# A gated mix of memory attention and a SiLU feed-forward: four v products on unscaled float32 operands, the last segment's q first, and two sets of scheduling prices

## The chip, the core and the metric

The kernel runs on one core of one Trainium2 chip. The metric is the device time of one execution in microseconds (us). Three executions of the kernel before took 552.75, 551.69 and 554.92 us; the median is 552.75 us.

The core has a matrix engine (TensorE, PE in the profile, with its weight loads listed as PEld), VectorE (DVE), ScalarE (ACT), GpSimd (POOL) and a queue engine that mostly issues transfers (SyncE, SP). Each engine works through its own instructions in the order in which they were written; semaphores make one engine wait for another.

## The reference

The input x has 2048 rows of 448 numbers. Two branches are computed from it and mixed row by row.

```python
q, k, v = x @ wq, x @ wk, x @ wv          # 16 heads of 28, 4 segments of 512 rows
for s in range(4):
    p = softmax(q[s] @ k[s].T / sqrt(28) + mask)
    a_dot = p @ v[s]
    a_mem = (phi(q[s]) @ M) / (phi(q[s]) @ z + 1e-6)     # phi(t) = t + 1 if t > 0 else exp(t)
    o[s] = sig(beta) * a_mem + (1 - sig(beta)) * a_dot
    M, z = M + phi(k[s]).T @ v[s], z + sum(phi(k[s]))
a = o @ wo
b = silu(x @ w1) @ w2                      # 1792 hidden columns
g = sigmoid((x * gate_w).sum(-1))
out = g * a + (1 - g) * b
```

Memory M and z are those of the segments before, so segment 0 has no memory to read and segment 3 does not write one.

## The kernel before

**Arithmetic.** PE multiplies 16-bit operands here. Every float32 operand is first multiplied by a power of two that fits its largest value and then split into a high 16-bit part and a low one, the remainder. The product is then three matmuls per 128 rows of the contraction (high·high, high·low, low·high). As the contraction is 448 = 3·128 + 64, and the 64 rows hold high and low stacked, one product of a tile is 3·3 + 2 = 11 matmuls. `halves` (L584) makes the two parts: the high part on ACT, or for the first segment and the weights on ACT or DVE (L590, L592), and the low part on DVE in one instruction (L579) or on POOL in two (L581, L582), of which the first scales the raw data in place. `product` (L604) issues the 11 matmuls, all of them on line L612.

**Scales.** A scale needs the size of the whole matrix first. For x and the weights of q, k and v it comes from sums of squares (`squares`, L432, on ACT) or largest values (`size`, L422, on DVE), one small float32 matmul over the partitions (L460, called a guard below), and a chain of four small DVE instructions (L464 to L468). The last of them writes `up`, which the high and low parts wait for.

**Stages.** First the loads and scales of x's first segment and of wv, wq and wk. While they arrive, PE runs matmuls on a zeroed tile that nothing reads: 8 of them (L791), then 37 more (L796, `MORE`), each of lowest priority. Then the projection stage: for 16 pairs of segment and group of four heads, `proj` (L893) makes q and k, `vproj` (L955) makes v in 16 tiles of 128 rows, `memory` (L996) accumulates M, and `retrieve` (L1031) reads it with float32 matmuls (L1044, L1045) for segments 1 to 3. After it the attention of all segments, with 10 of the 14 column blocks of the feed-forward in between as filler, and at last the output stage: the other four blocks, `@ wo`, the mix and the stores.

**Order.** The instructions of all engines are put in order while the program is built, by a list scheduler in the file (`Sched`, L146). Each task has an engine or a choice of two, an assumed duration, a priority and the PSUM banks or buffers that it takes; of all tasks that can go, the one that starts first goes, and ties on PE are settled by priority plus a price for weight loads that nothing covers (`PRICE`, `rank`, L214). Numbers at the head of the file (L37 to L91) set priorities. `SLACK` biases the choice between two engines. `LOCK` stands for DVE and POOL keeping each other out of a shared port. PSUM has eight banks, in three groups: mm (q and k), sc (v, transposes, scores) and cc (guards, memory, retrieval). A product takes the next bank of its group and cannot begin until the bank's last reader is done.

**Names.** `raw` holds wv and wq as loaded, `wa` here wk, `xraw` a tile of x; `wvs`, `wqs`, `wks` and `xh` are the split forms; `vt` a finished tile of v; `stg` a finished q or k; `pe`, `pp`, `ph` its steps through phi; `tqk`, `spk`, `rv` small scale factors; `amr` what retrieval gives.

## Time and profile before

| | |
|---|---|
| median of three runs | 552.75 us |
| the profiled execution's own time | 552.3 us |
| its span, first to last instruction | 550.6 us |
| outside the span | 1.7 us |
| PE, PEld busy | 540.9, 301.6 us |
| DVE, ACT, POOL busy | 403.2, 407.4, 336.7 us |
| granted PE clock, mean | 1.000 |

The span is what the prediction works in; the profiled execution is 0.45 us below the median, and 1.7 us lie outside its span. A timeline row gives the start in the span, the time until the last instruction of the row ended, the engine, the source line, what is written and read, and how many instructions the row merges; behind it in brackets stands the idle time ahead of it and what ended it. Instructions of one engine overlap at their ends, so what one costs in a row of many is the distance between starts, which is shorter than the duration in a row of one.

### The profile page before, as it was taken

Reading aid. Unit: us, or ns where it says so; the run is one execution under the profiler, and the core shown is the slowest. Engines: PE = TensorE matmul, PEld = TensorE weight load, DVE = VectorE, ACT = ScalarE, POOL = GpSimd, SP = SyncE. Lnnn points to the kernel's source line nnn. Section 1 sums busy time; section 2 is a strip of 40 time slices with the busy share of each in tenths; the row PEclk is TensorE's granted clock in tenths of the full one; section 3 lists DMA queues with packets and bytes.
Section 4 is the critical chain, followed back from the end, with each engine's and each line's share of the span. In section 5 each row is a group of like instructions: output and inputs, shape, how many; then the busy total and the mean of one; then the engine's idle time right before and its main releaser. Section 6 shows DMA issues by size and latency. Waiting matters only on the chain.

```text
span 550.6 us, 11673 instructions
## 1 busy us (share of the span) xinstructions
PE 540.9 (98%) x4087; PEld 301.6 (55%) x4087; DVE 403.2 (73%) x991; ACT 407.4 (74%) x698; POOL 336.7 (61%) x543
## 2 busy tenths in 40 slices
PE   8999999999999999999999999999999999999997
PEld 3455566556644556555565555565555555555544
DVE  5998999797869866778655789767897228864472
ACT  5996888595457988999887999879997897501140
POOL 3115525526623788888899988798989886211220
PEclk9999999999999999999999999999999999999999
DMA  8678578455467324332324334465301212689972
GB/s 309 230 227 251 175 214 230 145 147 169 137 183 188 110 77 118 104 88 69 101 73 119 87 85 137 128 134 141 106 9 47 86 52 62 227 197 247 257 202 69
DMA packets 78059, 78.94 MB, mean 143 GB/s; under 512 B 44040, under 2 KB 67720, under 8 KB 78000
## 3 DMA queue, kind: packets, MB, share of 16 engines
q1 hardware_dynamic: 77424, 77.21, 49.3%
q10 hardware_dynamic: 576, 0.99, 0.5%
q8 instruction: 32, 0.52, 0.4%
q14 instruction: 27, 0.22, 0.1%
HBM read 48.41 MB, written 26.09 MB: 135 GB/s over the span
## 4 chain that ended last, share of the span: by engine, by line
PE 92%; ACT 4%; DVE 2%; DMA 2%; issue 0%; DVEq 0%; ACTq 0%
PE mm L612 30%; PE mm L1192 17%; PE sc L612 11%; PE sc L717 6%; PE sc L1288 6%; PE cc L1192 6%; PE cc L1322 6%; PE cc L612 5%; ACT pf L1293 2%; PE cc L1044 1%; DMA raw<-in_wq_dram 1%; ACT phl L1305 1%; PE cc L1007 1%; PE sc L946 1%; PE sc L713 1%; DMA raw<-in_wv_dram 1%
## 5 line engine op out<-in xcount | busy, mean ns | idle before, releaser
L1309 POOL TENSOR_TENSOR phl<-pf,phl 128x384 f16<-128x384 f32 (+1 forms) x192 | 188.8, 1003 | 25.8 <-ACT phl L1305 25.7
L1293 ACT ACTIVATE pf<-sc,lift,es 128x512 f32<-128x512 f32 (+1 forms) x192 | 126.2, 706 | 13.2 <-PE sc L1288 10.8
L727 DVE CUSTOM_DVE_ANT_0 sc<-sc,mk 128x384 f32<-128x384 f32 (+1 forms) x192 | 105.6, 573 | 27.5 <-PE sc L717 25.3
L1192 PE MATMUL mm<-wb,ghl 128*128 128x448 f16 (+1 forms) x516 | 112.0, 348 | 0.0
L612 PE MATMUL mm<-xh,wa 128*128 128x512 f16 x429 | 107.0, 378 | 0.0
L1192 PEld LDWEIGHTS <-ghl 128*128 128x128 f16 x684 | 64.5, 97 | 51.0 <-issue 0.4
L1305 ACT ACTIVATE phl<-pf 128x1280 f16<-128x1280 f32 x64 | 81.4, 1272 | 14.3 <-POOL pf L1299 13.9
L612 PEld LDWEIGHTS <-wa 128*128 128x128 f16 x572 | 53.8, 97 | 54.7 <-issue 1.8
L1288 PE MATMUL sc<-ring 86*128 86x512 f16 (+3 forms) x256 | 62.5, 299 | 0.6 <-DVE mx L727 0.5
L717 PE MATMUL sc<-ring 84*128 84x128 f16 (+3 forms) x256 | 59.4, 299 | 0.7 <-ACT pf L1293 0.6
L1322 PEld LDWEIGHTS <-phl 128*128 128x128 f16 x1280 | 42.0, 96 | 10.1
L612 PE MATMUL mm<-xh,wqs 128*128 128x512 f16 x176 | 43.2, 379 | 0.8 <-DVE wqs L579 0.8
L1322 PE MATMUL cc<-vg,phl 128*128 128x29 f16 (+1 forms) x1280 | 43.7, 182 | 0.0
L623 POOL TENSOR_TENSOR ol<-ol,ml 128x448 f32<-128x448 f32 x12 | 13.6, 1136 | 46.9 <-DMA ol<-o_scr 37.2
L612 PE MATMUL mm<-xh,wks 128*128 128x512 f16 x176 | 41.9, 379 | 0.0
L1330 DVE TENSOR_REDUCE oraw<-cc 128x116 f32<-128x232 f32 x64 | 25.3, 396 | 20.6 <-PE cc L1322 20.4
L629 ACT ACTIVATE oh<-ol,os 128x448 f16<-128x448 f32 x16 | 10.7, 666 | 39.2 <-POOL ol L623 39.2
L612 PE MATMUL sc<-wvs,xh 128*128 128x450 f16 x176 | 37.8, 353 | 0.2 <-ACT xh L590 0.2
L1192 PE MATMUL cc<-wb,ghl 128*128 128x448 f16 x168 | 37.7, 352 | 0.0
L612 PE MATMUL cc<-xh,wa 128*128 128x512 f16 x143 | 36.5, 378 | 1.1 <-DVE amr L1050 1.1
L1288 PEld LDWEIGHTS <-ring 86*128 86x128 f16 x256 | 24.2, 97 | 23.0 <-issue 1.1
L612 PE MATMUL sc<-wos,oT 128*128 128x448 f16 x176 | 35.7, 352 | 0.0
(177 smaller groups left out, 920.8 us busy)
## 6 DMA issues: line engine op xcount, KB each, us to landing
rawf<-in_w_dram SPq DMA_DIRECT2D x26, 256.0 KB
rawf<-in_w_dram SPq DMA_DIRECT2D x28, 224.0 KB
v_scr<-vt SPq DMA_DIRECT2D x16, 232.0 KB
vg<-v_scr SPq DMA_DIRECT2D x16, 232.0 KB
xraw<-in_x_dram SPq DMA_DIRECT2D x14, 256.0 KB
q_scr<-stg SPq DMA_DIRECT2D x16, 224.0 KB
ring<-q_scr SPq DMA_DIRECT2D x16, 224.0 KB
k_scr<-stg SPq DMA_DIRECT2D x16, 224.0 KB
```

The source lines that it names most:

```text
L612: nc.tensor.matmul(ps(), *p[i], start=(i == 0), stop=(i == n - 1))
L623: d = pool(530, lambda: nc.gpsimd.tensor_add(b.v, b.v, m.v), d, e, uses=[b, m], **k)
L629: hi = copy(D + 110, lambda: nc.scalar.activation(half2.v[:, :D], ol.v, AF.Copy, scale=sc), *ready, takes=[half2], uses=[ol], prio=prio)
L717: nc.tensor.matmul(ps.v[:, u:u + n], rg.v[:KS, 0, hh, i * 128:(i + 1) * 128], rg.v[:KS, 1, hh, :n], start=(i > 0), stop=(i > 0 or j == 3), ...
L727: nc.vector.tensor_tensor_reduce(r, r, MK[:, L - n:], 1.0, NEG, OP.add, OP.max, mx.v[:, hh, i:i + 1])
L1192: nc.tensor.matmul(ps.v[:, lo:hi], g.v[:, y, sl], w.v[:, z, lo:hi], start=(j == 0 and i == 0), stop=(j == len(fs) - 1 and i == 2))
L1288: nc.tensor.matmul(ps.v[:, e:e + w], rg.v[:KK, 1, hh, j * 128:(j + 1) * 128], rg.v[:KK, 0, hh, j * 128:], start=True, stop=True)
L1293: ex.append(sact(e, lambda b=b, ps=ps, pf=pf, e=e: nc.scalar.activation(pf.v[:, b, :e], ps.v[:, :e], AF.Exp, bias=lift, scale=es[:, s:s + ...
L1305: hi = copy(1280, lambda hl=hl, flat=flat: nc.scalar.activation(hl.v[:, 0], flat(), AF.Copy), *mk, takes=[hl], uses=[pf], prio=p0 + 2)
L1309: low = pool(w - u + 22, lambda hl=hl, flat=flat, u=u, w=w: nc.gpsimd.tensor_sub(hl.v[:, 1, u:w], flat()[:, u:w], hl.v[:, 0, u:w]), low, u ...
L1322: nc.tensor.matmul(p[:, i, :2 - z], hl.v[:, z, u:u + 128], vg.v[:, j, hh, :2 - z], start=(z == zs[0] and i == 0), stop=(z == zs[-1] and j ...
L1330: nc.vector.tensor_reduce(orw.v[:, hh], p, axis=AX.X, op=OP.add)
```

## The change

There are three parts, and some smaller ones with them.

**The first four v products.** For the 128-row tiles 0 to 3 the product is done by `vearly`: four float32 matmuls on the unscaled `xraw` and `raw`, as soon as these have landed. Scale and remainder are taken afterwards, by the factor `rvf` that the copies out of PSUM multiply with. The loads are put in another order for that: on SP x tile 0, wv slices 1 and 3, x tile 2, on ACT's queue wv 0 and 2, x 1 and 3. 27 of the 37 low-priority matmuls go. `wvs`, the split form of wv, is still needed for segments 1 to 3, but later; its high parts are all made on ACT.

**The last segment.** Priorities of its q products and of its retrievals are lowered step by step with the group (`LASTQ`), so that they come ahead of its k and v.

**Prices in two stages.** `PRICE` and `SLACK` have one value in the projection stage and another (`PRICE2`, `SLACK2`) afterwards, and nearly all the numbers that set priorities have new values.

Beside these: x's first-segment low parts are bound to an engine (tile 0 to POOL, the others to DVE), squares are always taken on ACT, DVE's high parts count as users of the shared port and POOL's small instructions no longer do, and the very last output tile is cut 336 + 112 columns wide where it was 224 + 224.

```diff
-MORE = 37
+MORE = 10
...
-PRICE = 124.57
+PRICE = 249.08
+PRICE2 = 142.57
+SLACK2 = -0.34
...
-    def halves(j, hi, lo, dst, src, n, d, prio, takes=(), uses=(), both=False):
+    def halves(j, hi, lo, dst, src, n, d, prio, takes=(), uses=(), both=False, after=None, on=None):
...
-        return [h, scaled(n + 64 * (len(lo) - 1), low, h, uses=tuple(takes) + tuple(uses), prio=prio)]
+        if on:
+            eng, m = (pool, 2.2) if on == "POOL" else (dve, 1)
+            return [h, eng(m * (n + 64 * len(lo)), lambda: low(nc.gpsimd if on == "POOL" else nc.vector), h, after, port=on == "DVE",
+                           uses=tuple(takes) + tuple(uses), prio=prio)]
+        return [h, scaled(n + 64 * (len(lo) - 1), low, h, after, uses=tuple(takes) + tuple(uses), prio=prio)]
...
-            XC[s, c] = halves(NSEG - 1 - s, hi, lo, lambda: X16[s], src, L, d, prio, uses=[b], both=s == 0)
+            XC[s, c] = halves(NSEG - 1 - s, hi, lo, lambda: X16[s], src, L, d, prio, uses=[b], both=s == 0,
+                              after=EARLY[c][1] if s == c == 0 else None, on=("POOL" if c == 0 else "DVE") if s == 0 else None)
...
+        def vearly(k, prio):
+            ps, p, (xr, dx) = Buf(BK["sc" if k < 3 else "mm"]), None, XR[0, k]
+            for c in range(NC + 1):
+                wr, view, dw = RAWW["v", c]
+
+                def go(c=c, view=view):
+                    w = 128 if c < NC else REM
+                    nc.tensor.matmul(ps.v[:, :D + 2], xr.v[:w, c * 128:(c + 1) * 128], view()[:w], start=c == 0, stop=c == NC)
+                p = pe(quad(D + 2), go, p, dx, dw, takes=[] if c else [ps], uses=[ps, xr, wr], prio=prio)
+            EARLY[k] = ps, p
...
-            p = product(lambda: ps.v[:, :D + 2], pairs, D, prio, deps=need, cuts=cuts, takes=[ps], kind=half)
+            if k < NF:
+                ps, p = EARLY[k]
+                fit, turn, known = rvf, -1.0, RVF[0]
...
-            proj(t, "q", o)
+            proj(t, "q", o if s < NSEG - 1 else o - LASTQ * g)
...
-                retrieve(t, o + 8)
+                retrieve(t, o + 8 if s < NSEG - 1 else o + 8 - LASTQ * g)
...
+    sch.price, sch.slack = PRICE2, SLACK2
...
-            halves = [(0, D // 2), (D // 2, D)] if tail and tb == TB - 1 else [(0, D)]
+            halves = [(0, 3 * D // 4), (3 * D // 4, D)] if tail and tb == TB - 1 else [(0, D)]
```

The order in which instructions stand changes on every engine. Line numbers of the changed kernel differ (L460 becomes L468, L579 L587, L581 and L582 L589 and L590, L612 L624, L796 L808, L977 L1001, L1044 L1068, L1050 L1074). At the start PE had, ahead of the first v product, low-priority matmuls and the third guard's followers:

```order
L460 MATMUL cc_264<-sums,ones_73 128x5
...
L796 LDWEIGHTS maskb
L796 MATMUL mm_141<-maskb 128x512
L612 LDWEIGHTS xh_96
L612 MATMUL sc_295<-wvs,xh_96 128x450
...
L612 LDWEIGHTS wqs
L612 MATMUL mm_347<-xh_96,wqs 128x512
```

Now it has the float32 products there, with the four guards between them, and low-priority matmuls ahead of the first q product. Names with mm are in the mm banks; the last float32 product takes one of them, and the first k product (`mm_397`) is the next to take the same bank.

```order
L808 MATMUL mm_143<-maskb 128x512
L978 MATMUL sc_193<-raw_120,xraw 128x450 x4
L468 MATMUL cc_213<-sums,ones_73 128x5
L978 MATMUL sc_215<-raw_120,xraw 128x450 x4
L468 MATMUL cc_239<-sums,ones_73 128x5
L978 MATMUL sc_241<-raw_120,xraw 128x450 x2
L468 MATMUL cc_257<-sums,ones_73 128x5
L978 MATMUL sc_241<-raw_120,xraw 128x450 x2
L978 MATMUL mm_273<-raw_120,xraw 128x450 x4
L468 MATMUL cc_306<-sums,ones_73 128x5
```

So 44 16-bit matmuls of v are gone from behind the scales, and 16 float32 ones stand ahead of them. DVE, which makes the low parts, had this between the scale of x's first segment and that of wk (the chain L464 to L468 for wk stands behind it):

```order
L579 SCALAR_TENSOR_TENSOR xh_96<-xraw,up,xh_96 64x128
L579 SCALAR_TENSOR_TENSOR wqs<-raw_119,up,wqs 128x512 x3
L428 TENSOR_REDUCE sizes<-wqs 128x1
L579 SCALAR_TENSOR_TENSOR wqs<-raw_119,up,wqs 128x512
L428 TENSOR_REDUCE sums<-xraw 128x1 x3
L464 TENSOR_REDUCE few_123<-cc_379 128x1
```

The same place on DVE now, from the chain of wq's scale on:

```order
L476 RECIPROCAL up<-top 128x1
L1001 SCALAR_TENSOR_TENSOR vt_107<-sc_193,rvf,vt_107 128x16x28
L1001 SCALAR_TENSOR_TENSOR vt_108<-sc_215,rvf,vt_108 128x16x28
L441 TENSOR_REDUCE sums<-xraw 128x1
L472 TENSOR_REDUCE few_124<-cc_306 128x1
L473 TENSOR_SCALAR few_124<-few_124 128x1
L475 TENSOR_SCALAR top<-few_124 128x1
L476 RECIPROCAL up<-top 128x1
L587 SCALAR_TENSOR_TENSOR wqs<-raw_120,up,wqs 128x512 x4
L587 SCALAR_TENSOR_TENSOR wks<-wa,up,wks 128x512 x4
L1001 SCALAR_TENSOR_TENSOR vt_109<-sc_241,rvf,vt_109 128x16x28
L1001 SCALAR_TENSOR_TENSOR vt_110<-mm_273,rvf,vt_110 128x16x28
```

The low parts of wq moved behind the chain of wk's scale, and the copies that free the float32 products' banks stand at two places, the last of them behind all low parts of wq and wk. POOL had only small instructions in that part of the program:

```order
L516 TENSOR_SCALAR tqk<-top 128x1
L813 AFFINE_SELECT maskb<-maskb 128x128
L514 TENSOR_SCALAR tqk<-top 128x1 x2
L516 TENSOR_SCALAR spk<-up 128x1
L514 TENSOR_SCALAR spk<-spk 128x1
```

It now has the low part of x's tile 0 and, behind the small ones, those of wv's four slices, two large instructions for each:

```order
L524 TENSOR_SCALAR rvf<-up 128x1
L589 TENSOR_SCALAR xraw<-xraw,up 128x384
L590 TENSOR_TENSOR xh_97<-xraw,xh_97 128x3x128
L589 TENSOR_SCALAR xraw<-xraw,up 64x128
L590 TENSOR_TENSOR xh_97<-xraw,xh_97 64x128
L522 TENSOR_SCALAR tqk<-top 128x1 x2
L524 TENSOR_SCALAR spk<-up 128x1
L522 TENSOR_SCALAR spk<-spk 128x1
L825 AFFINE_SELECT maskb<-maskb 128x128
L589 TENSOR_SCALAR raw_120<-raw_120,up 128x450
L590 TENSOR_TENSOR wvs<-raw_120,wvs 128x450
```

This is work that moved from DVE to POOL. At the end of the projection stage DVE had the two reductions of the last retrieval directly ahead of the feed-forward's first work:

```order
L977 SCALAR_TENSOR_TENSOR vt_113<-sc_2118,vt_113 128x16x28
L989 TENSOR_SCALAR gate<-gate 128x4
L990 RECIPROCAL gate<-gate 128x4
L991 TENSOR_SCALAR ogate<-gate 128x4
L1050 TENSOR_REDUCE amr<-cc_2150 128x232
L1050 TENSOR_REDUCE amr<-cc_2158 128x232
L1055 RECIPROCAL amw<-amw 128x16
```

There now stand a v tile and a k product's remainder behind them:

```order
L1074 TENSOR_REDUCE amr<-cc_2062 128x232
L1074 TENSOR_REDUCE amr<-cc_2077 128x232
L1079 RECIPROCAL amw<-amw 128x16
L1001 SCALAR_TENSOR_TENSOR vt_114<-sc_2071,vt_114 128x16x28
L1013 TENSOR_SCALAR gate<-gate 128x4
L1014 RECIPROCAL gate<-gate 128x4
L1015 TENSOR_SCALAR ogate<-gate 128x4
L920 SCALAR_TENSOR_TENSOR stg<-mm_2096,stg 128x512
```

On PE, 8 matmuls of v and 11 of k now stand between the last retrieval and the first feed-forward matmul, where none stood before.

More of the change, by code (lines that the diff above doesn't have):

```diff
@@ L158, in __init__ @@
         self.tail = 1.0
+        self.price, self.slack = PRICE, SLACK
     def add(self, eng, dur, fn, deps=(), takes=(), uses=(), prio=0.0, lat=0.0, port=False):
@@ L200, in locked @@
     def locked(self, t, eng, s):
-        if eng == "POOL" or eng == "DVE" and t.port:
+        if eng == "POOL" and t.port is not None or eng == "DVE" and t.port:
             s = max(s, self.port["DVE" if eng == "POOL" else "POOL"] + LOCK)
@@ L249, in run @@
                 t.end = s + t.costs[t.eng]
-            if t.eng == "POOL" or t.eng == "DVE" and t.port:
+            if t.eng == "POOL" and t.port is not None or t.eng == "DVE" and t.port:
                 self.port[t.eng] = t.end
@@ L434, in squares @@
         at, junk = place(j), Buf(JUNK[0])
[L436 to L443 removed]
+        SIZE[j].append(copy(n + 200 - 45, lambda: nc.scalar.activation(junk.v[:, :n], view(), AF.Square, accum_out=at), *deps,
+                            takes=[junk], uses=uses, prio=prio))
     def total(j, view, n, *deps, uses=(), prio):
@@ L509, in few @@
     def few(n, fn, *deps, **k):
-        return sch.add("POOL", 0.33 * n, fn, deps, **k)
+        return sch.add("POOL", 0.33 * n, fn, deps, port=None, **k)
     def by(o, i, a, b=None, op0=OP.mult, op1=OP.mult):
@@ L965, in pairs @@
-            def pairs():
-                p = passes(W["v"], X16[s][:, :, tb * 128:(tb + 1) * 128], True)
-                return [p[i] for i in order]
-            p = product(lambda: ps.v[:, :D + 2], pairs, D, prio, deps=need, cuts=cuts, takes=[ps], kind=half)
+            v = Buf(VT)
+            if k < NF:
+                ps, p = EARLY[k]
+                fit, turn, known = rvf, -1.0, RVF[0]
+            else:
+                ps = Buf(BK["sc"])
+                p = product(lambda: ps.v[:, :D + 2], lambda: passes(W["v"], X16[s][:, :, tb * 128:(tb + 1) * 128], True), D, prio,
+                            deps={c: WS["v"][c] + XC[s, c if s else tb] for c in range(NC + 1)}, takes=[ps], kind=half)
+                fit, turn, known = FIT, tqk[:, 3 * s + 2:3 * s + 3], VREADY[s]
```

122 lines of the change are left out of this document (61 added, 61 removed).

## Prediction

> **What bounds the kernel now.** I read the totals first, then the chain that ended last, then busy time by stretches, and at last what PE waits for.
>
> ```profile
> span 550.6 us, 11673 instructions
> PE 540.9 (98%) x4087; PEld 301.6 (55%) x4087; DVE 403.2 (73%) x991; ACT 407.4 (74%) x698; POOL 336.7 (61%) x543
> ...
> PE 92%; ACT 4%; DVE 2%; DMA 2%; issue 0%; DVEq 0%; ACTq 0%
> ```
>
> PE is busy for 540.9 of 550.6 us and carries 92% of the chain. Only two things can move the time: a change in PE's work, and the 9.7 us in which PE idles. The stretches show where those lie (columns: length, then busy us of PE, PEld, DVE, ACT and POOL).
>
> ```profile
> core 0: us, PE busy (x) PEld busy (x) DVE busy (x) ACT busy (x) POOL busy (x), PEclk, DMA share, GB/s
> 15.00:20.00 5.00, 4.20 (x21) 1.88 (x21) 4.74 (x12) 5.00 (x11) 0.95 (x2) 1.00 0.72 245
> 30.00:35.00 5.00, 5.00 (x27) 2.36 (x26) 4.90 (x13) 5.00 (x10) 1.46 (x6) 1.00 0.80 242
> 130.00:160.00 30.00, 28.61 (x171) 16.97 (x169) 20.76 (x41) 13.74 (x28) 16.78 (x34) 1.00 0.46 136
> 160.00:200.00 40.00, 38.80 (x278) 20.28 (x277) 33.65 (x84) 33.85 (x53) 21.53 (x30) 1.00 0.57 155
> 540.00:551.00 11.00, 6.89 (x49) 4.46 (x46) 2.86 (x5) 0.00 (x0) 0.00 (x0) 0.97 0.16 54
> ```
>
> PE idles 1.4 us at 130 to 160, 1.2 us at 160 to 200 and some 4 us in the tail; at 30 to 35 not at all, though DVE and ACT have almost no slack there. The granted clock is 1.00, so durations can be compared across stages. What ended the idle time after 60 us (matmul, what released it, us in all, count, longest):
>
> ```profile
> PE cc L612 <- DVE amr L1050: 1.1, 1, 1.1
> PE sc L717 <- ACT pf L1293: 0.6, 2, 0.3
> ...
> PE cc L1045 <- DVE phq L935: 0.3, 1, 0.3
> ```
>
> The first and the last belong to the last retrieval, ahead of the feed-forward. At the start, "busy" hides what counts, because PE runs matmuls that nothing reads. There the order of PE has to be read.
>
> ```profile
> 4.37 2.97 PE L796 MATMUL mm<-maskb 128*128 128x512 bf16 x13
> 7.26 0.39 PE L460 MATMUL cc<-sums,ones 128*128 128x5 f32 x2
> ...
> 11.46 0.39 PE L460 MATMUL cc<-sums,ones 128*128 128x5 f32 x2 [0.99 <-DVE sums L459]
> ...
> 15.13 3.98 PE L612 MATMUL sc<-wvs,xh 128*128 128x450 f16 x20 [0.22 <-ACT xh L590]
> 18.95 0.38 PE L612 MATMUL mm<-xh,wqs 128*128 128x512 f16 x1
> ...
> 20.14 2.58 PE L612 MATMUL mm<-xh,wqs 128*128 128x512 f16 x11 [0.81 <-DVE wqs L579]
> ```
>
> Until 15.13 us PE does nothing that is needed but guards. From 15.13 to 18.95 it does 20 of the first segment's 44 v matmuls, then waits for wq's low part, and from 20.14 on it has work without a gap. So the kernel's PE time is counted from 20.14: what must still be done then, plus the stalls behind it.
>
> **The change part by part.** *A, the removed v matmuls.* 44 go, but 20 of them ran before 20.14, in time that q could not use. So 24 are saved.
>
> ```profile
> 49.98 2.10 PE sc L612 x11
> ```
>
> This link of the chain is one product of 11 matmuls: 2.10 / 11 = 0.191 us each. A is −24 × 0.191 = −4.6 us.
>
> *The float32 products.* There is no float32 matmul with 450 columns before. The nearest rows are retrieval's, with 232 and 116 columns (starts, not lengths, are read):
>
> ```profile
> L460 PE MATMUL cc<-sums,ones 128*128 128x5 f32 x14 | 2.3, 234 | 1.3 <-DVE sums L459 1.0 <-ACT junk L438 0.3
> ...
> 127.61 0.46 PE L1044 MATMUL cc<-mhl,phq 112*128 112x232 f32 x1
> 127.91 0.22 PE L1045 MATMUL cc<-mhl,phq 112*128 112x116 f32 x1
> 127.97 0.33 PE L1044 MATMUL cc<-mhl,phq 112*128 112x232 f32 x1
> 128.13 0.22 PE L1045 MATMUL cc<-mhl,phq 112*128 112x116 f32 x1
> 128.19 0.26 PE L1007 MATMUL cc<-vt,phk 128*112 128x232 f16 x1
> ```
>
> A float32 matmul leaves two records (14 for seven guards, whose pairs take 2.3 / 7 = 0.33 us each). A record of 232 columns takes 128.13 − 127.97 = 0.16 us, one of 116 columns 0.06, so 450 columns give an estimate of 0.16 + 218 × 0.10 / 116 = 0.35, and two records 0.70 us per matmul. The bounds are 0.38 (two records at the 16-bit 0.19) and 1.03 (0.70 and a guard's whole pair on top, for weight loads that nothing covers); I take 0.70, worked out from the same kind of instruction. Sixteen cost 11.2 us and the four guards between them 1.3. When they can begin is seen on ACT, which starts on wv's first slice as it lands:
>
> ```profile
> 4.41 0.58 ACT L438 ACTIVATE junk<-raw 128x450 bf16<-128x450 f32 x1 [0.25 <-DMA raw<-in_wv_dram]
> ```
>
> With 0.4 us for x's first tile to follow, they go from about 4.8 to about 17.3 if no later load is late. They take the place of idle time and of the 27 unread matmuls (13 take 2.97 us), ahead of 20.14. The cover ends where DVE wants wk's guard, 18.8 less the guard and its way, so about 1.0 us is to spare; beyond it each 0.1 us on the price costs 1.6 us.
>
> *B, when q can start.* That is DVE's walk. Its rows:
>
> ```profile
> 10.89 0.45 DVE L592 TENSOR_SCALAR wvs<-raw,up 128x450 f16<-128x450 f32 x1
> 15.24 4.06 DVE L579 SCALAR_TENSOR_TENSOR xh<-xraw,up,xh 128x384 f16<-128x384 f32 x8
> 19.32 2.08 DVE L579 SCALAR_TENSOR_TENSOR wqs<-raw,up,wqs 128x512 f16<-128x512 f32 x3
> 22.31 1.87 DVE L428 TENSOR_REDUCE sums<-xraw 128x1 f32<-128x512 f32 x3
> 24.09 0.15 DVE L464 TENSOR_REDUCE few<-cc 128x1 f32<-128x5 f32 x1
> 24.65 0.17 DVE L468 RECIPROCAL up<-top 128x1 f32<-128x1 f32 x1
> 24.73 0.61 DVE L977 SCALAR_TENSOR_TENSOR vt<-sc,vt 128x448 f16<-128x448 f32 x1
> 25.25 0.68 DVE L904 SCALAR_TENSOR_TENSOR stg<-mm,stg 128x512 f16<-128x512 f32 x1
> ```
>
> From them: a chain is 24.65 + 0.17 − 24.09 = 0.73 us, the low part of a tile of x 4.06 / 4 = 1.02, one of wq or wk 2.08 / 3 = 0.69, a v low 25.25 − 24.73 = 0.52, a reduction 1.87 / 3 = 0.62. x's guard was at 11.46; a high of wv (0.45) no longer stands ahead of it on DVE, a few float32 matmuls do on PE, so I take 11.2. With guard (0.39) and chain the scale is there at 12.3. Two highs of x on DVE, which the removed high shows at 0.45 for 450 columns, take until 13.3, three lows of x until 16.4, wq's chain until 17.1, two v lows until 18.2, one reduction until 18.8, wk's chain until 19.5. In before q's run of eleven began 0.82 us after the first low of wq (20.14 − 19.32), so now at 20.35: +0.2 us.
>
> That sum leaves out the low parts that POOL now makes.
>
> ```profile
> 149.40 0.94 POOL L1059 TENSOR_TENSOR am<-amr,amw 128x448 f32<-128x448 f32 x1
> 169.01 1.42 POOL L581 TENSOR_SCALAR rawf<-rawf,up 128x448 f32<-128x448 f32 x1 [12.80 <-ACT wb L590]
> 170.51 1.04 POOL L582 TENSOR_TENSOR wb<-rawf,wb 128x448 f16<-128x448 f32 x1
> ...
> 70.26 0.68 DVE L935 TENSOR_TENSOR phq<-ph,phq 112x512 fp32r<-112x512 f32 x1
> 149.76 1.14 DVE L935 TENSOR_TENSOR phq<-ph,phq 112x512 fp32r<-112x512 f32 x1
> ```
>
> The same DVE instruction took 0.68 us alone and 1.14 us when POOL's started 0.36 ahead of it: 0.46 of the 0.58 us that POOL still ran came on top. On POOL a low part is 1.42 + 1.04 = 2.46 us; x's tile 0, cut into 384 and 64 columns, is by width, with some 0.2 for a short instruction, 2.8 us, and all five are 12.6 us. DVE could lose anything from nothing (DVE first in the port, or reading PSUM) to all of it. I take half, since which of the two starts first is open at each instruction: 1.4 us for x's tile 0, where DVE makes x's other lows. q then starts at 21.75, and B is +1.6 us.
>
> The Trainium skill speaks against this part: "SBUF — State Buffer", section "SBUF: two separate sides", says that the pair of ports shared by VectorE and GpSimd is an exclusive lock, so that a VectorE instruction with two SBUF inputs and a GpSimd instruction reading SBUF block each other fully. The trace agrees with it at 149.76 (1.14 against 0.68). By the page alone, whoever starts first decides, and a DVE that always came second would lose all of the 12.6 us, the third rival below.
>
> *C, the first k product.* Its bank is freed by the fourth v low, behind eight lows and another v low. From 19.5: 8 × 0.69 + 2 × 0.52 = 6.6, so 26.1. PE is through with two q products by about 20.35 + 4.75 = 25.1 (22 × 0.216, the 33 of a later row taking 7.12 together). With the port both move by 1.4, and the first low of wv on POOL, which falls among the eight, adds half of 2.46 to DVE: 28.7 against 26.5, C is +2.2 us; without the port +1.0. The other three lows of wv (7.4 us of POOL) come behind the second copy of q on ACT, not before 28 us. There DVE has 0.1 us in 5 to spare, but also four lows of wv and one of x fewer than before, 4 × 0.69 × 450 / 512 + 1.0 = 3.4 us, nearly half of 7.4; I take nothing, with 0 and 7.4 as the ends.
>
> *D, the end of the projection.* Behind the last retrieval there now stand 8 v and 11 k matmuls, some 4 us of PE work, over DVE's two reductions. That covers the waits of 1.1 and 0.3: −1.4 us. The ends are −1.4 and 0, if another wait comes there.
>
> *E, the rest.* Retrieval's blocks are entered from 16-bit work 24 times instead of 20; an entry costs 0.30 (127.61 to 127.91) against 0.16 inside, +0.14 × 4 = +0.55 us. Squares on ACT, the loads' order and the prices change no other PE work ahead of the attention: 0, hidden by PE's run without a gap. The last output tile ends on a copy of 112 columns instead of 224.
>
> ```profile
> 546.93 0.81 DVE L1403 SCALAR_TENSOR_TENSOR y<-mm,ogs,ya 128x224 f32<-128x224 f32 x2 [1.62 <-PE mm L1192]
> ```
>
> Half of a 0.4 us copy is 0.2 less, while its 24 matmuls keep their number and their columns in all: I take 0, within 0.3.
>
> The sum is −4.6 + 1.6 + 2.2 − 1.4 + 0.55 = −1.65 us on the profiled execution's 552.3, so 550.65. The median of the runs shown is 0.45 above that execution: 551.1 us.
>
> **The rivals.** Half a per cent, 2.76 us, is about what a measurement of this kernel tells from no change: 549.99 and 555.51 are the limits.
>
> *The port costs nothing* (faster). POOL's lows fall where DVE waits for guards or reads PSUM. Then B is +0.2 and C +1.0, the sum −4.25, the time 548.5 us. For it: DVE's walk has two chains and two PSUM readers in it, and a DVE that is already in the port delays POOL, which nothing waits for. Against it: three lows of x stand together, with 95% of 15 to 20 us busy. It is below the limit from a DVE loss of about 1.5 us instead of 2.6.
>
> *POOL's lows fall on DVE* (slower). If more than half of the 12.6 us lands and PE runs dry, k and the first memory products wait. The limit is passed with 4.4 us more than my 2.6, so from 7.0 of the 12.6 us; at ten of them the time is 551.1 + 7.4 = 558.5. For it: DVE has 0.1 us of slack in 30 to 35. Against it: the late lows have no reader before segment 1, and DVE's load falls by 3.4.
>
> *The float32 matmul is dear* (slower). With 1.2 us each they end at 4.8 + 16 × 1.2 + 1.3 = 25.3, 8.0 later, less 1.0 of cover: 551.1 + 7.0 = 558.1. It decides from 0.70 + (4.4 + 1.0) / 16 = 1.04, just above my bound of 1.03. Late loads would do the same from 5.4 us.
>
> *D does nothing* (no change): the wait moves to another block, 552.5 us.
>
> **How the numbers follow.** The forecast of 551.1, with D's other end and half of C's in it 549 to 554, has a chance of 0.43, of which 0.04 lie below 549.99 and 0.01 above 555.51; D failing is part of it. The port at nothing has 0.32, POOL's lows on DVE 0.18, dear or late float32 products 0.06, and 0.01 is left for others. Faster is 0.32 + 0.04 = 0.36, slower 0.18 + 0.06 + 0.01 = 0.25, the same 0.39. For the range, the low end is 548.5 less 1.2 (the wait at 160 to 200 gone as well) and 0.8 for A, should fewer v matmuls have counted as done: 546.5. The high end, 557.0, takes in a loss of 8.5 of the 12.6 us and leaves about 0.1 above.
>
> **What the profile after would show.** A: no 16-bit v product before segment 1. The float32 products: 32 records of 450 columns between 5 and 18 us, 0.35 from start to start; wrong if above 0.5, or if PE waits for loads between them past 18. B: the first run of q matmuls at 21 to 22.5; wrong below 20.6 or above 24. The port: DVE's lows (0.69 and 1.02 here) stretched beside POOL's new instructions; none stretched means the faster rival. C: PE's first k matmul waits 1 to 2.5 us for a v low. D: no wait for the retrieval's reductions, and none over 0.5 us in its place. The prediction fails above all by the port, and next by a stall at 30 to 60 us that the trace of before has no row for.

## The result, and the profile after

The changed kernel takes 554.02 us (median of twelve executions, 551.23 to 554.85) against 552.65 us for the kernel before in the same rounds (551.69 to 554.92): a ratio of 1.0011, with a 95% interval of 0.9992 to 1.0029. That is no difference. The forecast was 551.1 us, a gain of 0.3%, which its own bound of 0.5% counts as no change; the measured median lies in its range (546.5 to 557.0). What follows is less about the sum than about its terms, several of which were off, nearly all of them to the slow side.

The profiled execution took 554.45 us, its span 552.3, so 1.74 us more than the span before (552.29 against 550.55, unrounded). The spans of the twelve executions lie between 549.0 and 552.7 us, so the profiled one is near their upper end, and the account below is that of one execution. From the page:

```profile
span 552.3 us, 11603 instructions
PE 540.8 (98%) x4048; PEld 300.4 (54%) x4048; DVE 398.1 (72%) x983; ACT 407.0 (74%) x697; POOL 365.6 (66%) x559
```

PE is busy for as long as before, POOL for 29 us more, DVE for 5 less. What PE waited for (us in all, count, longest):

```profile
PE mm L624 <- ACT wvs L598: 2.3, 1, 2.3
PE cc L1220 <- DVE ghl L1203: 1.1, 1, 1.1
...
PE mm L624 <- DVE stg L920: 0.8, 1, 0.8
...
PE mm L624 <- DVE wqs L587: 0.4, 1, 0.4
```

The waits at the end of the projection are gone. In their place there are two ahead of the first k products and one of 1.1 us near the end. The start on PE, in order of time:

```profile
5.27 3.72 PE L978 MATMUL sc<-raw,xraw 128*128 128x450 f32 x8 [0.61 <-DMA xraw<-in_x_dram]
...
9.16 3.46 PE L978 MATMUL sc<-raw,xraw 128*128 128x450 f32 x8
12.55 0.39 PE L468 MATMUL cc<-sums,ones 128*128 128x5 f32 x2
...
19.82 0.39 PE L468 MATMUL cc<-sums,ones 128*128 128x5 f32 x2
...
22.58 4.71 PE L624 MATMUL mm<-xh,wqs 128*128 128x512 f16 x21 [0.41 <-DVE wqs L587]
29.61 2.54 PE L624 MATMUL mm<-xh,wks 128*128 128x512 f16 x11 [2.33 <-ACT wvs L598]
32.93 2.54 PE L624 MATMUL mm<-xh,wks 128*128 128x512 f16 x11 [0.78 <-DVE stg L920]
```

A float32 product of four matmuls takes 12.55 − 9.16 = 3.4 us, 0.85 us a matmul where 0.70 was taken. The guard of x's scale stands behind eight of them, at 12.55 instead of the 11.2 of the working, and q's run begins at 22.58 (before: 20.14). Then PE waits 2.33 and 0.78 us for k. DVE over the same stretch:

```profile
14.56 4.07 DVE L587 SCALAR_TENSOR_TENSOR xh<-xraw,up,xh 128x384 f16<-128x384 f32 x6
...
21.74 2.81 DVE L587 SCALAR_TENSOR_TENSOR wqs<-raw,up,wqs 128x512 f16<-128x512 f32 x4
24.47 3.90 DVE L587 SCALAR_TENSOR_TENSOR wks<-wa,up,wks 128x512 f16<-128x512 f32 x4
...
28.89 0.67 DVE L1001 SCALAR_TENSOR_TENSOR vt<-mm,rvf,vt 128x448 f16<-128x448 f32 x1
...
32.20 0.68 DVE L920 SCALAR_TENSOR_TENSOR stg<-mm,stg 128x512 f16<-128x512 f32 x1
```

Three low parts of x take as long as four did before (4.07 against 4.06 us), and wk's four 3.90 us against 2.81 for wq's. The copy of the fourth v product ends at 29.56, and the first k product starts at 29.61: the wait named after ACT in the table ends with DVE. The copy of the first q product ends at 32.88, and the second k product starts at 32.93. Beside DVE's long ones stands POOL:

```profile
14.39 1.37 POOL L589 TENSOR_SCALAR xraw<-xraw,up 128x384 f32<-128x384 f32 x1
15.85 0.91 POOL L590 TENSOR_TENSOR xh<-xraw,xh 128x384 f16<-128x384 f32 x1
16.86 0.79 POOL L589 TENSOR_SCALAR xraw<-xraw,up 64x128 f32<-64x128 f32 x1
17.73 0.74 POOL L590 TENSOR_TENSOR xh<-xraw,xh 64x128 f16<-64x128 f32 x1
...
24.00 1.87 POOL L589 TENSOR_SCALAR raw<-raw,up 128x450 f32<-128x450 f32 x1
25.95 1.21 POOL L590 TENSOR_TENSOR wvs<-raw,wvs 128x450 f16<-128x450 f32 x1
```

The account in spans, from PE's records one by one (work is the span from the start of q's run less the idle time and less the 3.7 us behind the last matmul):

| term | forecast | measured |
|---|---|---|
| A and E, PE's work behind q's start (524.1 → 520.3) | −4.05 | −3.8 |
| B, start of q's run (20.14 → 22.58) | +1.6 | +2.4 |
| C, waits for the first k products (0 → 2.33 + 0.78) | +2.2 | +3.1 |
| D, waits at the end of the projection (1.39 → 0) | −1.4 | −1.4 |
| waits at 160 to 200 us (1.17 → 0.53) | 0 | −0.6 |
| waits at 80 to 100 and behind 200 us (0 → 1.75), and idle pieces under 0.08 us each (+0.2) | 0 | +2.0 |
| sum in the span | −1.65 | +1.7 |
| time outside the span (1.7 → 2.15) | 0 | +0.45 |

### The profile page after: what moved, and what is told of

The parts are those of the page before. It is cut to its first block, busy times and chain, and to the rows that moved or that the text cites. A ratio compares the mean times of both kernels' runs of the same rounds, so it can differ in the third digit from the quotient of the medians.

```text
span 552.3 us, 11603 instructions
## 1 busy us (share of the span) xinstructions
PE 540.8 (98%) x4048; PEld 300.4 (54%) x4048; DVE 398.1 (72%) x983; ACT 407.0 (74%) x697; POOL 365.6 (66%) x559
## 4 chain that ended last, share of the span: by engine, by line
PE 68%; ACT 10%; DVE 9%; DMA 7%; issue 2%; POOL 1%; SPq 1%; DVEq 0%; POOLq 0%; ACTq 0%
PE mm L624 20%; PE mm L1220 14%; PE sc L729 5%; PE sc L1316 5%; PE sc L624 5%; PE cc L1350 5%; PE cc L1220 4%; ACT pf L1321 4%; PE cc L624 3%; DMA ol<-o_scr 3%; ACT phl L1333 2%; DMA pl<-p_scr 1%; PE sc L978 1%; DMA rawf<-in_w_dram 1%; PE cc L1068 1%
## 5 line engine op out<-in xcount | busy, mean ns | idle before, releaser
L1321 ACT ACTIVATE pf<-sc,lift,es 128x512 f32<-128x512 f32 (+1 forms) x192 | 128.1, 713 | 15.6 <-PE sc L1316 14.4
L1220 PE MATMUL mm<-wb,ghl 128*128 128x448 f16 (+2 forms) x516 | 111.2, 348 | 0.0
L624 PE MATMUL mm<-xh,wa 128*128 128x512 f16 x429 | 107.9, 378 | 0.0
L624 PEld LDWEIGHTS <-wa 128*128 128x128 f16 x572 | 53.7, 97 | 54.5 <-issue 2.0
L729 PE MATMUL sc<-ring 84*128 84x128 f16 (+3 forms) x256 | 56.8, 299 | 0.7 <-ACT pf L1321 0.3
L624 PE MATMUL mm<-xh,wks 128*128 128x512 f16 x176 | 43.5, 379 | 3.1 <-ACT wvs L598 2.3
L624 PE MATMUL mm<-xh,wqs 128*128 128x512 f16 x176 | 42.1, 379 | 0.4 <-DVE wqs L587 0.4
L624 PE MATMUL cc<-xh,wa 128*128 128x512 f16 x143 | 37.0, 378 | 0.3 <-DVE ghl L1203 0.3
L1327 POOL TENSOR_SCALAR_AFFINE_SELECT pf<-pf 128x384 f32<-128x384 f32 x64 | 34.3, 536 | 2.5 <-ACT pf L1321 1.6
L624 PE MATMUL sc<-wos,oT 128*128 128x448 f16 x176 | 35.6, 352 | 0.0
```

What stands on the lines that cost most here:

```text
L624: nc.tensor.matmul(ps(), *p[i], start=(i == 0), stop=(i == n - 1))
L729: nc.tensor.matmul(ps.v[:, u:u + n], rg.v[:KS, 0, hh, i * 128:(i + 1) * 128], rg.v[:KS, 1, hh, :n], start=(i > 0), stop=(i > 0 or j == 3), ...
L1220: nc.tensor.matmul(ps.v[:, lo:hi], g.v[:, y, sl], w.v[:, z, lo:hi], start=(j == 0 and i == 0), stop=(j == len(fs) - 1 and i == 2))
L1321: ex.append(sact(e, lambda b=b, ps=ps, pf=pf, e=e: nc.scalar.activation(pf.v[:, b, :e], ps.v[:, :e], AF.Exp, bias=lift, scale=es[:, s:s + ...
L1327: mk.append(pool(204, lambda pf=pf: nc.gpsimd.affine_select(pf.v[:, :, :128], pf.v[:, :, :128], [[0, 3], [1, 128]], OP.is_ge, 0.0, base=0, ...
```

## The experiments

All times below come with five rounds beside the kernel before. Where nothing else is said, a kernel has exactly the instructions of the changed kernel, in its recorded order on every engine, with only the named ones moved; lines and names are the changed kernel's. "q" is the start of the second q matmul, "k waits" are PE's waits from there to 50 us. Both, and the span, are those of the one profiled execution. Where there are twelve executions of a kernel, they spread over 2.5 to 7.6 us (e7, e8 and f4 have six), so whether a kernel is faster is read from the ratio.

| kernel | q | k waits | span | ratio to before (95%) |
|---|---|---|---|---|
| changed | 22.58 | 2.33 + 0.78 | 552.3 | 1.0011 (0.9992–1.0029) |
| e1_guard | 22.13 | 2.07 | 551.0 | 0.9994 (0.9977–1.0011) |
| e2_bank | 23.00 | 3.27 | 552.6 | 1.0024 (0.9999–1.0048) |
| e3_wv0late | 22.67 | 1.16 + 0.08 | 551.2 | 0.9977 (0.9964–0.9991) |
| e4_x0dve | 22.36 | 1.53 + 0.14 | 548.9 | 0.9981 (0.9964–0.9999) |
| e5_bank_dve | 23.14 | 1.99 | 552.8 | 1.0001 (0.9983–1.0019) |
| e6_unqueue | 22.38 | 1.00 + 2.41 | 551.9 | 1.0019 (1.0002–1.0036) |
| e7_nf2 | 23.31 | 0 | 555.5 | 1.0093 (1.0070–1.0116) |
| e8_before_lastq | 20.09 | 0 | 556.5 | 1.0076 (1.0056–1.0095) |
| f1_port | 22.54 | 1.15 + 0.09 | 549.7 | 0.9988 (0.9973–1.0002) |
| f2_port_guard | 21.79 | 1.16 + 0.08 | 549.2 | 0.9987 (0.9972–1.0002) |
| f3_fill | 22.83 | 0.17 + 0.78 | 554.1 | 1.0037 (1.0016–1.0059) |
| f4_lastq0 | 22.63 | 2.33 + 0.78 | 583.8 | 1.0588 (1.0562–1.0615) |

### The guard of x's scale

```diff
 L468 MATMUL cc<-sums,ones 128x5
-L978 MATMUL sc_215<-raw,xraw 128x450 x4
+L978 MATMUL sc_215<-raw,xraw 128x450 x3
 L468 MATMUL cc<-sums,ones 128x5
+L978 MATMUL sc_215<-raw,xraw 128x450
```

> The changed kernel in its own order of instructions, with one float32 matmul moved: the last of the second v product stands behind the guard of x's scale instead of ahead of it. Theory (q starts late because that guard stands behind eight float32 matmuls that cost 0.87 us each instead of the 0.70 predicted, and because of the port): the guard goes from 12.55 to about 11.4 us, where DVE's sums are ready, and x's scale, DVE's low parts and the first run of q follow by 0.8 to 1.1 us (22.58 to about 21.6); the span falls by 0.8 to 1.1 us if the waits behind q stay as they are. Rival (DVE's own work and wk's guard, behind all sixteen float32 matmuls at 19.8 us, set the start of q): q starts within 0.3 us of 22.58 and the span stays.

PE in order of time:

```profile
11.73 0.28 PE L468 MATMUL cc<-sums,ones 128*128 128x5 f32 x2
...
20.19 1.89 PE L808 MATMUL mm<-maskb 128*128 128x512 bf16 x8
21.91 4.91 PE L624 MATMUL mm<-xh,wqs 128*128 128x512 f16 x22
28.89 6.59 PE L624 MATMUL mm<-xh,wks 128*128 128x512 f16 x22 [2.07 <-DVE vt L1001]
```

The guard went to 11.73, and DVE's first low part of wq from 21.74 to 21.02. q's run gained less, 0.45 us, because its first matmul now follows without a gap on the eight unread matmuls behind wk's guard: PE's own queue is the next bound. So the first theory holds in direction with half its size; the waits for k fell by 1.0 us too (3.11 to 2.07), as DVE's whole queue began earlier. wk's guard, the rival's bound, held DVE up by no more than 0.2 us. The 22 matmuls of k took 6.59 us, 1.4 more than in e3 below (5.15), at about half the granted clock; more on that at the end.

### The bank, or DVE's queue

```diff
-ps = Buf(BK["sc" if k < 3 else "mm"])
+ps = Buf(BK["sc" if k < 3 else "cc"])
```

> The changed kernel in its own order, with the fourth float32 product in a bank of the guards' group (cc) instead of one of q's and k's (mm). Bank theory, the prediction's: the 2.33 us wait ahead of the first k product is for that bank alone; it shrinks to about 0.3 us, the 0.78 us wait behind it stays, and the span falls by about 2 us. Queue theory: DVE is behind with everything, and the second k product needs the bank of the first q product, whose copy stands in DVE's queue behind the same v copies, the gate and two reductions and ends at 32.9 us; the first k product starts earlier, the second no earlier than 32.9 us, the wait there grows by what the first loses, and the span stays within 0.3 us.

```profile
27.54 2.54 PE L624 MATMUL mm<-xh,wks 128*128 128x512 f16 x11
33.35 4.22 PE L624 MATMUL mm<-xh,wks 128*128 128x512 f16 x11 [3.27 <-DVE stg L920]
```

The first k product begins without a wait, and the second waits 3.27 us, as much as both did together (3.11). So the bank theory falls. The next run takes the copies of q ahead as well (DVE's rows, behind wk's low parts):

```diff
+L920 SCALAR_TENSOR_TENSOR stg<-mm_333,stg 128x512
+L920 SCALAR_TENSOR_TENSOR stg<-mm_341,stg 128x512
 L1001 SCALAR_TENSOR_TENSOR vt_109<-sc_241,rvf,vt_109 128x16x28
 L1001 SCALAR_TENSOR_TENSOR vt_110<-cc_273,rvf,vt_110 128x16x28
...
-L920 SCALAR_TENSOR_TENSOR stg<-mm_333,stg 128x512
 L441 TENSOR_REDUCE sums<-xraw 128x1
-L920 SCALAR_TENSOR_TENSOR stg<-mm_341,stg 128x512
```

> The bank of the run before, and in DVE's queue the copies of the two q products directly behind wk's low parts, ahead of the last two v copies, the gate and three reductions. Queue theory: now both waits go, the first k product runs as wk's low parts come (27.3 us), the second follows at about 29.7 us, the 3.1 us of waits shrink to 0.5 or less, and the span falls by 2 to 2.8 us, unless the reductions that now come later delay the scale of x's second segment (37.8 us) and a wait appears there. Bank theory: no more than the 2 us of the bank alone.

```profile
27.68 4.91 PE L624 MATMUL mm<-xh,wks 128*128 128x512 f16 x22
...
37.27 3.79 PE L624 MATMUL mm<-xh,wks 128*128 128x512 f16 x9 [1.99 <-DVE stg L920]
```

Both k products run through, as queue theory had it, but a wait of 1.99 us comes three products later, again for a copy on DVE: the waits fell by 1.1 us instead of 2.6 or more, and the span, for which 2 to 2.8 us less was expected, did not fall (552.8). The last of this line puts six reductions behind the low parts of x's second segment as well, together with the moves of e1, e3 and e5.

> The changed kernel in its own order, with the moves of the runs before together (the guard of x's scale one float32 matmul earlier, POOL's first low part of wv last, the fourth float32 product in a bank of cc, the copies of q ahead of v's, the gate and reductions in DVE's queue), and six reductions of DVE that the third segment of x and later scales need put behind the low parts of x's second segment. Queue theory (whatever bank is freed, PE waits until DVE's backlog of the start is worked off, so only work taken out of DVE's queue or out of POOL's way helps): the first run of q starts at 22.0, the waits between 22 and 90 us fall from 3.3 to 0.5 or less, the span goes from 552.3 to 549 (less up to 1.1 where the wait at 534 us does not happen), and the median lies 0.4 to 0.8% below the kernel before. Rival: the waits return at 40 to 90 us because the reductions stand there now, and the span stays above 551.

```profile
35.31 2.10 PE L624 MATMUL mm<-xh,wks 128*128 128x512 f16 x9 [1.00 <-DVE stg L920]
...
48.30 0.60 PE L962 MATMUL sc<-ident,ph 112*128 112x112 f32 x4 [2.41 <-DVE ph L945]
```

The rival was right: 3.4 us of waits, at 34 and 46 us, and the span is 551.9. The changed kernel's stretches (columns as in the prediction's):

```profile
30.00:35.00 5.00, 4.22 (x20) 1.86 (x19) 4.93 (x11) 0.96 (x3) 4.82 (x5) 1.00 0.67 193
35.00:40.00 5.00, 5.00 (x28) 2.57 (x26) 5.00 (x10) 4.29 (x10) 0.98 (x1) 1.00 0.61 160
```

DVE is busy for 9.93 of these 10 us; another order of its queue only chose which product waits.

### The port of DVE and POOL

In e3 POOL makes the low part of wv's first slice last of the four, so that its first large instruction there begins at 28.66 us, past DVE's work on wk.

> The changed kernel in its own order, but POOL makes wv's first low part last instead of first of the four, so that POOL has no large instruction beside DVE's low parts of wk. Port theory: those four take 4 x 0.70 = 2.8 us instead of 3.8 (0.74 each, none of 1.1 or 1.5), the first k product starts about 1.0 us earlier (28.6 instead of 29.6) and the second about as much; the span falls by 0.7 to 1.0 us. Rival (the two long ones are long for another reason, PSUM or the weights' layout): they stay at 1.1 and 1.5 us and nothing moves.

```profile
24.56 2.73 DVE L587 SCALAR_TENSOR_TENSOR wks<-wa,up,wks 128x512 f16<-128x512 f32 x4
```

wk's four low parts took 2.73 us instead of 3.90, all at 0.74. The k waits fell by 1.9 us (3.11 to 1.24), more than the 1.0 expected, since the gate's small instructions on DVE, which stand ahead of q's copies, had been stretched too (0.55 and 0.82 us, now 0.15 and 0.52). This is the one kernel whose ratio lies clearly below 1 (0.9977), though the plain medians, 552.60 against 552.95 us of the kernel before, are only 0.06% apart.

In e4 it is x's tile 0.

```diff
-on=("POOL" if c == 0 else "DVE") if s == 0 else None
+on="DVE" if s == 0 else None
```

> The changed kernel in its own order, with the low part of x's tile 0 on DVE, behind the other three, and no longer on POOL. Port theory: three lows beside POOL took 4.07 us, so four of them without it take about 4 x 1.02 = 4.1 us; DVE's chain for wq starts at 18.7 as before and the first run of q within 0.3 us of 22.6: moving that part to POOL had bought nothing. Rival (POOL takes work off DVE, and the lows were long for another reason): DVE needs 5.1 to 5.4 us, and q starts 1.0 to 1.3 us later, at 23.6 to 23.9.

```profile
14.47 3.96 DVE L587 SCALAR_TENSOR_TENSOR xh<-xraw,up,xh 128x384 f16<-128x384 f32 x8
```

Four low parts alone on the port are quicker (3.96) than three beside POOL (4.07), and q's run begins at 22.36: giving that part to POOL bought nothing. As POOL's later work shifted, wk's low parts also fell from 3.90 to 3.15 us, and the k waits to 1.67, which I had not expected.

Both moves together, and then with e1's:

> The changed kernel in its own order with both moves out of POOL's way: x's tile 0 has its low part on DVE, and POOL makes wv's first low part last of the four. If the port is what the start lost, the two gains add: the first run of q at 22.4 as with the first move alone, wk's four low parts 0.74 us each, the waits for k 1.0 us or less in all (3.1 in the changed kernel, 1.7 and 1.2 with one move each), no stretch at half the granted clock, and the span 1 to 2.5 us below the changed kernel's 552.3; against the kernel before a ratio of 0.995 to 0.998. Rival (the waits for k are for DVE's copies whatever POOL does): no better than one move alone, 0.998.

> The run before with the guard of x's scale one float32 matmul earlier as well. That guard moved q's start by 0.45 us, with a wait of 2.07 us behind it that brought half the clock. With the port free the wait should be about 1.2 to 1.5 us and the clock stay at 1.00; q starts at about 21.9, and as wk's low parts come earlier by as much, the span falls by another 0.3 to 0.5 us. Rival (wk's guard behind all sixteen float32 matmuls then sets the start): no gain, or half of that.

The first k product in f1:

```profile
28.40 5.15 PE L624 MATMUL mm<-xh,wks 128*128 128x512 f16 x22 [1.15 <-DVE vt L1001]
```

The gains in k waits do not add: about 1.2 us is left in both, as in e3, for the copy of the fourth v product, with wk's four low parts at 2.73 us. That is DVE's plain work. In f2 q begins 0.75 us earlier than in f1, and the span is 0.5 us shorter. Neither is told apart from e3 or e4 by its time (0.9988 and 0.9987, both intervals reach 1.000), so the expected 0.995 to 0.998 did not come. All four medians (552.60, 552.24, 551.83, and 552.4 for f2) lie 1.4 to 2.2 us below the changed kernel's 554.02, measured in other rounds. One of f2's twelve executions took 1980 us, for which its record shows no cause; the comparison leaves it out.

### Fewer float32 products

```diff
-NF = 4
+NF = 2
```

> The changed kernel with two float32 products instead of four (its scheduler makes the order anew, so all later stages may differ by some tenths). 22 16-bit matmuls of v come back, 6 of them ahead of q. If a removed v matmul is worth its full 0.191 us (the prediction's term A), the work behind q's start grows by 16 x 0.191 = 3.1 us and the span by 2 to 3 us. Queue theory: v's matmuls fill time in which PE waited for DVE (3.1 us in the changed kernel), so the waits behind q shrink by about as much as the work grows, and the span stays within 1 us of 552.3.

```profile
17.42 0.36 PE L624 MATMUL sc<-wvs,xh 128*128 128x450 f16 x1 [1.97 <-DVE xh L587]
18.32 0.39 PE L468 MATMUL cc<-sums,ones 128*128 128x5 f32 x2 [0.53 <-ACT junk L449]
20.25 1.30 PE L624 MATMUL sc<-wvs,xh 128*128 128x450 f16 x3 [1.54 <-DVE vt L1001]
...
23.31 4.52 PE L624 MATMUL mm<-xh,wqs 128*128 128x512 f16 x13 [1.33 <-DVE wqs L587]
```

Half of each theory held. No wait is left from q's start to 80 us, as queue theory said. But the span grew by 3.2 us: PE's work behind q is 4.5 us more, of which 16 v matmuls are 3.1 and the half clock of about 20 to 26 us some 1.6 (13 q matmuls in 4.36 us from the first start to the next row's, instead of 13 × 0.216 = 2.8). What is left, 2.9 us for 16, agrees with the full 0.19 us for a removed matmul. The waits only moved ahead of q, which begins 0.7 us later.

### The last segment's priorities

e8 is the kernel before with that part alone, f4 the changed kernel without it; for both the scheduler makes the whole order anew.

```diff
-proj(t, "q", o)
+proj(t, "q", o if s < NSEG - 1 else o - 5.08 * g)
...
-retrieve(t, o + 8)
+retrieve(t, o + 8 if s < NSEG - 1 else o + 8 - 5.08 * g)
```

> The kernel before with the last segment's priorities alone (q and retrieval lowered by 5.08 per group). Term D of the prediction: the waits of 1.08 and 0.31 us at the end of the projection (150 to 153 us) go, the start up to 130 us is as before (first run of q at 20.1, no wait to 130 us), and the span falls by 1.0 to 1.4 us, to about 549.4. Rival: the waits only move to the k and v products that now come last, and the span stays.

PE's waits from 140 to 160 us, and then POOL in order of time:

```profile
PE cc L1044 <- POOL mhl L1027: 4.6, 1, 4.6
```

```profile
152.09 0.94 POOL L1059 TENSOR_TENSOR am<-amr,amw 128x448 f32<-128x448 f32 x1
...
154.51 0.43 POOL L1027 TENSOR_TENSOR mhl<-macc,mhl 112x116 fp32r<-112x116 f32 x1
```

Neither expectation held. The start is as before, but the retrieval, drawn forward, waits 4.62 us for the memory it reads: `mhl` stands in POOL's queue behind `am` and five scale factors. The span grew by 5.9 us, 3.5 of them in waits and 2.5 in PE's own work, as the clock stood at 0.50 from 154 to 160 us.

```diff
-LASTQ = 5.08
+LASTQ = 0.0
```

> The changed kernel with the step of the last segment's priorities set to zero (its scheduler makes the order anew); the last retrieval then stands directly ahead of the feed-forward's first matmuls again. Term D: the waits of 1.08 and 0.31 us of before come back at that place, 1.0 to 1.4 us in all. Rival (D came from the other new numbers, since the step alone gave the kernel before a wait of 4.6 us): no wait over 0.5 us at that place.

PE's waits from 140 to 160 us:

```profile
PE cc L1068 <- ACT phq L949: 1.6, 1, 1.6
PE cc L1069 <- DVE phq L951: 0.4, 1, 0.4
PE cc L624 <- DVE amr L1074: 0.4, 1, 0.4
```

Without the step the retrieval again stands last, and 2.3 us of waits are there, two thirds more than term D. So it seems that D needs the step, and that the step pays only together with the other numbers; as both kernels have a whole new order, no run shows this apart from the rest. The other 29 us of this run lie in the attention stage, some 20 of them in slower work and 9 in waits (columns as in the prediction's stretches):

```profile
220.00:225.00 5.00, 4.09 (x45) 2.42 (x41) 3.29 (x12) 2.84 (x6) 4.64 (x7) 1.00 0.32 76
...
230.00:235.00 5.00, 4.68 (x32) 2.22 (x32) 2.91 (x10) 4.93 (x8) 4.77 (x8) 0.50 0.04 11
```

The clock was at 0.50 from about 226 to 267 us, behind a stretch in which PE idled 0.91 of 5 us in pieces of up to 0.6. Which move of the new order brought that about was not tried.

### The clock

> The changed kernel in its own order with ten matmuls that nothing reads between the second q product and the first k product, in a free bank of cc; they last 2.2 us and end before the first k product can begin (29.6). In the runs with moved instructions the clock fell to 0.50 for some 3 us behind a wait of 2.1 to 3.3 us of PE, and in a part of the changed kernel's own executions the mean clock was 0.997. If the wait brings that about, none of these executions has a mean clock under 0.999, and the median is 0.3 to 1 us lower than the changed kernel's with no change in any wait but that one. Rival (the clock has nothing to do with the wait): about a third of the executions stay at 0.997.

Eleven of the twelve executions have mean clocks of 0.999 or 1.000. The profiled one has 0.998, and its half clock lies behind 552 us, where PE has no work left. So the first part holds in substance. But as only 3 of the changed kernel's 12 executions were at 0.997, this run alone does not show that the wait is the cause. The second part does not hold: the median is 555.95 us, 1.9 above the changed kernel. The filled wait is 0.17 us as meant, and q and k stand 0.25 us later than in the changed kernel. Most of the difference stands at 522 to 537 us, where PE waits 2.5 us in all (1.1 in the changed kernel). The waits of PE there, then DVE's row at one late load, and the same row of the changed kernel:

```profile
PE cc L1223 <- DVE ghl L1206: 1.3, 2, 0.9
...
PE cc L1223 <- ACT ghl L1204: 0.9, 1, 0.9
```

```profile
528.67 0.68 DVE L1430 SCALAR_TENSOR_TENSOR ya<-sc,gas,pl 128x448 f32<-128x448 f32 x1 [1.50 <-DMA pl<-p_scr]
```

```profile
526.80 0.68 DVE L1427 SCALAR_TENSOR_TENSOR ya<-sc,gas,pl 128x448 f32<-128x448 f32 x1
```

DVE stands here at a late load with the feed-forward's last copies behind it; in the changed kernel it waits as long for such loads in all (4.5 against 4.4 us from 500 to 540), but not at this place. In the kernels with the same order at that place this wait of PE was 0 (e1, e4, e6) to 1.1 us. Why it is longer here stays open.

## Why the prediction was right or wrong

**In its range, for the wrong balance.** Its class (no change) and its range held. The sign did not come out: the median went 1.4 us up, with an interval that includes no change. The errors did not cancel. In the profiled span they add up to 3.4 us (B 0.8, C 0.9, A and E 0.25, the later stages 1.4), and a range 10.5 us wide took them in. That the time stayed within half a per cent was in part luck.

**A and E were right together**: −3.8 for −4.05 us, and e7 agrees with A's price of a v matmul.

**B was 0.8 us short, by the price of a float32 matmul.** The price was asked about the wrong place. It was hidden behind wk's guard, as the step says (19.82, and DVE came for it at 21.1), but x's guard stands behind eight of the matmuls, and there 0.85 instead of 0.70 us, and a start at 5.27 instead of 4.8, made it 1.35 us late, of which shorter highs of x and a smaller loss to the port won back some 0.5. In e1, with seven ahead of it, the guard came at 11.73. The row scaled by columns gave 0.35 a record; it is 0.42 (3.4 us for eight).

**The port was sized well.** The step took half of POOL's time, 1.4 and 1.2 us. The runs show 1.1 (4.07 less three of 3.96 / 4 each) and 1.2 (3.90 less 2.73). The Trainium skill ("SBUF — State Buffer", "SBUF: two separate sides") calls the pair of ports an exclusive lock; e3 and e4 agree. Its extreme, that all of POOL's work lands on DVE, did not come: beside the three low parts past 28 us DVE's copies out of PSUM and its reductions kept their length (0.67 each), and only the gate's two small instructions grew.

**C had its size nearly (3.1 for 2.2) and its mechanism half.** The first k product did wait for the copy of the fourth v product, 2.33 us. Of the 3.1 us, 1.2 were DVE's plain work (f1; forecast 1.0), and 1.9 went with POOL's part (e3; forecast 1.2). But it was no wait for one bank that another bank would cure: e2 moved it whole to the next product, e5 and e6 to later ones. Most of the missing 0.9 us is the second wait, 0.78 us for q's copy behind the gate and two reductions, which the step did not look for. The prediction had named a stall at 30 to 60 us as its second risk.

**D was right in size, and only together with the rest**: alone (e8) it is a loss.

**The later stages had a zero that did not hold.** E puts all other changes ahead of the attention at nothing, "hidden by PE's run without a gap", and there only 0.15 us of new waits came beside those of C. For what comes behind, where the order is new too, the sum has no term but the last output tile: 1.6 us of new waits stand there, and 0.6 us of old ones at 160 to 200 us are gone. The largest, 1.10 us near the end, is partly the port again (DVE, then POOL, in order of time):

```profile
533.11 1.27 DVE L1249 SCALAR_TENSOR_TENSOR gf<-th,hsum 128x512 f32<-128x512 f32 x1
```

```profile
532.70 1.14 POOL L635 TENSOR_TENSOR ol<-ol,ml 128x448 f32<-128x448 f32 x1 [2.25 <-DVE ghl L1203]
```

The DVE instruction takes 0.69 us undisturbed. But that wait varies between profiles of kernels with the same order at that place (0 to 1.1 us, f3 apart), so one profile does not make it the change's.

**Of the rivals**, "the port costs nothing" is refuted by e3 and e4: the low parts got shorter as POOL moved away. In time both were worth 1.4 to 1.8 us of the median against the changed kernel, which brings them to the kernel before or 0.2% below it. "POOL's lows fall on DVE" needed 7.0 us of loss; e3 and e4 put it near 3 (1.9 of k waits and 1.1 ahead of q). "The float32 matmul is dear" needed 1.04 us; the price, 0.85, stays within its bounds (0.38 and 1.03). "D does nothing" is refuted by D's place, where no wait is left.

## What to carry to other kernels

When work moves to another engine to relieve a busy one, price it at both ends: here POOL's low parts cost DVE 2.3 us in the 15 us that mattered, and one of the two gave DVE nothing in return. When a wait sits behind an engine that is hardly ever idle (here 0.07 of 10 us), freeing the buffer that the wait names can just move it to the next buffer (e2). What shortened it here was other work out of that engine's way (e3, e4), or an earlier start of its queue (e1). A price hidden at its end can still be open in the middle: look for whatever else stands behind the costly instructions in the same queue.

## What the runs showed of the hardware

In three profiles a wait of PE of 2.0 to 3.3 us (e5, e1, e2) was followed, 0.2 to 1.1 us after its end, by half the clock for 3.4 us. The stretches of e1, whose wait of 2.07 us ended at 28.89:

```profile
28.00:30.00 2.00, 1.11 (x6) 0.52 (x6) 1.93 (x7) 1.73 (x5) 1.80 (x2) 1.00 0.76 266
30.00:32.00 2.00, 2.00 (x6) 0.65 (x5) 2.00 (x4) 0.23 (x2) 2.00 (x2) 0.51 0.70 199
```

It does not come each time: the changed kernel's profile has 2.33 us and a clock of 1.00 throughout, yet 3 of its 12 executions have a mean of 0.997. Counting executions at 0.997 or lower: with a longest wait of 1.5 to 3.3 us before 50 us (changed, e1, e2, e4, e5, e6) 30 of 72, with 1.2 us or less (e3, f1, f2, f3) none of 48. f3 differs from the changed kernel in that wait's filling alone. But the kernel before has them too, 23 of 87 (10 of 35, 8 of 23 and 5 of 29 in three sets of rounds), with no wait over 1.1 us in its profile; no trace of such an execution shows where. So the counts go with the early wait, and that it is the cause, or the only one, is not shown. The Trainium skill ("TensorE: Matmul & The Clock Gate", "Part 1: The HAM clock gate (the "warmup" mystery)") tells of a clock halved after an idle window of about 3.4 us that runs freely. That it comes in some executions and not in others agrees. The gap does not: here half the clock stood behind gaps of 2.0 and 2.07 us (e5, e1), and the measurement decides.

Secondly, the time outside the span was 1.6 to 1.8 us in the kernel before, e8 and e4, and 1.8 to 2.3 us in the other kernels. That is 0.45 us of the changed kernel's profiled time, and what sets it was not tried.
